# Attention, routing and two expert layers in one kernel: router logits of 19 of 24 chunks as fp16 products of rows turned by DMA, and preceding tokens counted per group

## The chip, the cores and the metric

One Trainium2 chip; the kernel runs on one of its cores. The metric is the device time of one execution in microseconds (us). A change of about 0.5% is what a measurement of this kernel can tell from none.

## The reference, cut to what matters

Gated linear attention over 4 batches, 8 heads, 768 steps and head size 48, then a mixture of 8 experts of which every token takes its best two by noisy logits, then a dense two-layer block. The change concerns `logits`, `noise_scale` and the places that the chosen tokens get in their expert's list.

```python
f = 1.0 / (1.0 + np.exp(-f_logit))
for t in range(S):
    state = f[:, :, t, :, None] * state + np.einsum('bhd,bhe->bhde', k[:, :, t], v[:, :, t])
    y[:, :, t] = np.einsum('bhd,bhde->bhe', q[:, :, t], state)
...
logits = x @ w_gate
noise_scale = np.log1p(np.exp(x @ w_noise))
noisy_logits = logits + noise_scale * noise
top2 = np.argpartition(-noisy_logits, 2, axis=1)[:, :2]
...
h = np.maximum(x[mask] @ w1[e], 0.0)
out[mask] += top2_w[mask, k, None] * (h @ w2[e])
...
h = x @ w_in
g = h - np.tanh(h)
return (g @ w_out).astype(np.float32)
```

## The kernel before, in words

The 3072 tokens are 24 chunks of 128 tokens: chunk j is step c = j // 4 of batch b = j % 4. The kernel has three stages. The first, some 180 us long, runs the attention chunk by chunk, routes the tokens and writes their rows into a DRAM list `xs` by expert. The second runs the experts from there, the third the dense block. The change lies in the first stage, and the order of all work there is written out by hand: each engine executes its instructions in the order in which the program issues them, and waits in place.

One pass of the main loop (`for j in range(NT)`) issues, in this order:

- `load_all(j + 3)`: on SP's queue the loads of `kq` (512 KB), `v` (192 KB) and, two chunks further ahead, `f` (256 KB); in passes 1 to 4 two `clear` writes of 288 KB each go behind them.
- `scores(j + 1)`: 8 fp32 products into two banks, and on DVE the masked copies `am` (L341).
- `scaled(j + 2)`: on ACT two exponentials (L320, L321), on DVE `kqT` for the keys (L323), on POOL `kqT` for the queries (L325).
- `post(...)`: on POOL two scatters (L479) of rows of chunks that are already routed; a scatter writes 128 rows of `x16`.
- `decay(j + 3)`: ACT (L310, L311) and on DVE the scan (L312).
- `logits(j - 1)` (L410): three fp32 products of `xT` with the two 16-column gate matrices (96 columns are streamed), and a copy of 16 columns to `lgs` on ACT (L411). If j - 1 is the last chunk of its group, `route` of that group is started as a generator.
- `outputs(j)`: 12 fp32 products into `pY` (L364, L366); ACT copies `pY` twice, to `x` in fp32 (L369) and to the high half of `x16` in fp16 (L371); DVE forms the low half from `x` and the high half (L372).
- `key_rows(j + 1)`, `states(j)` (L383, DVE L387, POOL L390).
- `x_transposed(j)`: three fp32 transposes of `x` on TensorE (L398) and a copy to `xT` on ACT (L400).
- between these, `advance(2)` takes two steps of the oldest started `route`; every second pass loads and splits a block of expert weights (`raw`, L144, L145).

`route` works on a group of four chunks (the last two groups have three and one): ACT makes the noise scale, DVE the best two per token and the mark `sel`; then `pre[:, j + 1]` adds up the marks of all chunks before, one small DVE addition per chunk (L440); two products on TensorE (L444, L445) give each token's place; more small DVE operations give the slots `yslot`, and 8 scatters are put on the list of `post`.

```python
for j in js:
    yield
    tt(pre[:, j + 1], pre[:, j], sel[:, j], op=OP.add)
for _ in range(2 if g < len(groups) - 2 else 1):
    yield
pos = ps.tile([128, 4, NE], F32, name="pt", tag="b7" if g > 4 else "b2")[:, :G]
nc.tensor.matmul(pos, before, sel[:, jj], start=True, stop=False)
nc.tensor.matmul(pos, ones, pre[:, jj], start=False, stop=True)
```

In the third stage `put_m` (L624) turns a 128 x 768 fp16 block by one DMA transpose from SP's queue, which is the shape that the change uses in the first stage. "Pass j" below is the j-th turn of the main loop; in the trace it is taken from the start of `scores(j + 1)` on TensorE to that of `scores(j + 2)`.

Of the kernel before, what the change touches and what calls it, by code (L numbers as in the profile page):

```python
# [23 lines left out]
NT = B * NCH  # L24
# [21 lines left out]
SM = 2.0 ** 12  # L46
SI = 2.0 ** 6
# [6 lines left out]
ISUM = (8.0, 1.0e8)  # L54
MSUM = (40.0, 1.0e9)
# [16 lines left out]
def fast(ctx, tc, flag, f_cols, kq_cols, v_rows, gates, blank, w12, w_in, w_out, out):  # L72
# [49 lines left out]
    pre = consts.tile([128, NT + 1, NE], BF, name="pre")  # L122
    nc.vector.memset(pre[:, 0, :], 0.0)

# [125 lines left out]
    with ExitStack() as actx:  # L250
# [106 lines left out]
        def outputs(j):  # L357
# [10 lines left out]
            x = work.tile([128, DM], F32, name="x")  # L368
            nc.scalar.activation(x, pY[:, :384], AF.Copy)  # L369
            x16 = xkeep[j // 4 % 3][:, j % 4, :]  # L370
            nc.scalar.activation(x16[:, :DM], pY[:, :384], AF.Copy, scale=SX)  # L371
            nc.vector.scalar_tensor_tensor(x16[:, DM:], x, SX, x16[:, :DM], op0=OP.mult, op1=OP.subtract)  # L372
            T["x", j], T["x16", j] = x, x16
# [20 lines left out]
        def x_transposed(j):  # L394
            x = T.pop(("x", j))
# [9 lines left out]
        group_of = {j: g for g, js in enumerate(groups) for j in js}  # L405
        def logits(j):
            p = ps.tile([128, 96], F32, name="pt", tag="b7")
            xT = T.pop(("xT", j))
            for a in range(3):
                nc.tensor.matmul(p, xT[:, a, :], gn[:, 16 * a:16 * a + 96], start=(a == 0), stop=(a == 2))  # L410
            nc.scalar.activation(lgs[:, j, :], p[:, :16], AF.Copy)  # L411
# [3 lines left out]
        def route(g):  # L415
# [5 lines left out]
            tt = nc.vector.tensor_tensor  # L421
            nl = small.tile([128, 4, NE], F32, name="nl")[:, :G]
# [15 lines left out]
            for j in js:  # L438
                yield
                tt(pre[:, j + 1], pre[:, j], sel[:, j], op=OP.add)  # L440
            for _ in range(2 if g < len(groups) - 2 else 1):
# [3 lines left out]
            nc.tensor.matmul(pos, ones, pre[:, jj], start=False, stop=True)  # L445
# [48 lines left out]
        warm(90)  # L494
        decay(0)
# [8 lines left out]
        decay(2)  # L504
        warm(30)
        for j in range(NT):
# [12 lines left out]
            if j:  # L519
                logits(j - 1)  # L520
                if j - 1 in ends:
                    chains.append(route(group_of[j - 1]))
# [7 lines left out]
            states(j)  # L530
            x_transposed(j)
# [193 lines left out]
    okay = consts.tile([128, 14], F32, name="okay")  # L725
# [17 lines left out]
    def checks():  # L743
# [4 lines left out]
        check(1, dv, 0.0, OP.is_lt)  # L748
        yield
# [3 lines left out]
        nc.tensor.matmul(count[:, 0], ones, pre[:, NT], start=True, stop=True)  # L753
        nc.tensor.matmul(count[:, 1], ones, pre[:, EARLY], start=True, stop=True)
        nc.tensor.matmul(count[:, 2], ones, pre[:, 4], start=True, stop=True)
# [365 lines left out]
```

## Time and profile before

| | |
|---|---|
| time, median of 3 runs | 971.24 us (967.05 to 971.27) |
| the profiled execution | 962.48 us, of which the span of the trace is 960.7 us |
| TensorE (PE) busy | 938.4 us, 98% |
| VectorE (DVE) busy | 616.0 us, 64% |
| ScalarE (ACT) busy | 611.2 us, 64% |
| GpSimd (POOL) busy | 160.5 us, 17% |
| DMA | 120.03 MB, mean 125 GB/s |
| passes 1 to 3 of the loop | 5.3 us each |
| passes 4 to 19 | 6.2 us each (scores at 33.64 to scores at 133.16) |

Shares over the whole span are averages over three stages with different limits, so the first stage has to be read by itself, and there by pass. The busy time of TensorE is modelled at its end, so that pass lengths are taken from starts of instructions.

### The profile page before, as it was taken

The page shows a single profiled execution, that of the slowest core. Times are in us where ns is not written, and L with a number is a line of the kernel's source. Part 1 is how long each engine was busy: PE and PEld are TensorE (multiplying, and loading weights), DVE is VectorE, ACT ScalarE, POOL GpSimd, SP SyncE. Part 2 cuts the span into 40 slices and gives each one's busy share as a digit, 9 for nine tenths or more (in the row PEclk, how much of TensorE's full clock was granted, in tenths as well). Part 3 has the DMA queues.
Part 4 walks back from the last instruction along what each step waited for, and adds up shares of the span by engine and source line. Part 5 has one row for each costly group of instructions (what it writes and reads, how often), then busy time and mean ns, then how long its engine had stood idle before and what let it go on. Part 6 is the DMA issues. An engine that isn't in the chain of part 4 may idle for free.

```text
span 960.7 us, 16309 instructions
## 1 busy us (share of the span) xinstructions
PE 938.4 (98%) x5970; PEld 576.5 (60%) x5970; DVE 616.0 (64%) x1274; ACT 611.2 (64%) x1593; POOL 160.5 (17%) x194
## 2 busy tenths in 40 slices
PE   8999998999999999999999999979999999999996
PEld 8999986555656565656556554535555555555553
DVE  8999995466464646566666556556566565665764
ACT  7777763575757575776767566666665666666663
POOL 2387786000000000000000223200301201000000
PEclk9999999999999999999999999989999999999999
DMA  7877855756565456564645354212222121110001
GB/s 274 286 248 252 263 166 170 200 176 167 153 177 149 161 143 187 151 157 134 186 122 136 99 149 103 64 34 44 74 42 47 44 58 42 42 26 1 33 1 37
DMA packets 111801, 120.03 MB, mean 125 GB/s; under 512 B 66400, under 2 KB 89568, under 8 KB 111584
## 3 DMA queue, kind: packets, MB, share of 16 engines
q1 hardware_dynamic: 105568, 100.03, 36.4%
q0 software_dynamic: 6144, 18.88, 6.3%
q8 instruction: 48, 0.79, 0.3%
q14 instruction: 41, 0.34, 0.1%
HBM read 76.41 MB, written 29.88 MB: 111 GB/s over the span
## 4 chain that ended last, share of the span: by engine, by line
PE 60%; ACT 21%; DVE 14%; issue 1%; DMA 1%; POOL 0%; SPq 0%; DVEq 0%; ACTq 0%
PE py L200 24%; PE ph L185 23%; ACT s L638 6%; DVE s L639 6%; DVE g L641 6%; ACT hs L647 5%; ACT z L637 5%; PE pY L366 4%; PE pA L339 2%; PE pt L410 2%; PE pY L364 2%; PE pK L383 2%; ACT junk L628 1%; ACT junk L149 1%; ACT g L614 1%
## 5 line engine op out<-in xcount | busy, mean ns | idle before, releaser
L200 PE MATMUL py<-wsplit,hs 128*128 128x384 f16 x2432 | 433.8, 327 | 7.2 <-ACT o L665 5.6
L200 PEld LDWEIGHTS <-hs 128*128 128x128 f16 x2432 | 237.0, 98 | 181.3 <-issue 9.2
L185 PE MATMUL ph<-xt,wsplit 128*128 128x512 f16 (+3 forms) x1152 | 223.5, 339 | 0.4 <-DMA xt<-xs 0.4
L185 PE MATMUL ph<-xt,winS 128*128 128x512 f16 x864 | 201.7, 379 | 0.0
L185 PEld LDWEIGHTS <-wsplit 128*128 128x128 f16 x1152 | 112.5, 98 | 86.7 <-DMA xt<-xs 0.8
L218 DVE SCALAR_TENSOR_TENSOR hs<-ph,hs 128x256 f16<-128x256 f32 (+2 forms) x192 | 79.6, 443 | 119.1 <-ACT hs L210 118.9
L608 POOL DMA_INDIRECT g<-y_rows,yslot x48 | 52.7, 1097 | 585.1 <-ACT wsplit L144 376.0
L210 ACT ACTIVATE hs<-ph 128x512 f16<-128x512 f32 (+3 forms) x128 | 65.8, 514 | 132.6 <-PE ph L185 132.6
L647 ACT ACTIVATE hs<-g 128x512 f16<-128x512 f32 x96 | 60.4, 629 | 138.5 <-DVE g L641 138.5
L185 PEld LDWEIGHTS <-winS 128*128 128x128 f16 x864 | 84.4, 98 | 92.0
L639 DVE SCALAR_TENSOR_TENSOR s<-s,z 128x512 f32<-128x512 f32 x96 | 66.5, 692 | 80.9 <-ACT s L638 80.9
L648 DVE TENSOR_TENSOR hs<-g,hs 128x512 f16<-128x512 f32 x96 | 66.4, 692 | 63.3 <-ACT hs L647 61.9
L145 DVE SCALAR_TENSOR_TENSOR wsplit<-raw,wsplit 128x768 f16<-128x768 f32 x72 | 70.3, 976 | 16.3 <-ACT wsplit L144 15.0
L149 ACT ACTIVATE junk<-wsplit 128x384 f16<-128x384 f16 x144 | 74.4, 516 | 2.3
L638 ACT ACTIVATE s<-z,bias_a 128x512 f32<-128x512 f32 x96 | 69.3, 722 | 3.1
L641 DVE SCALAR_TENSOR_TENSOR g<-s,ph 128x512 f32<-128x512 f32 x96 | 65.9, 687 | 3.3
L144 ACT ACTIVATE wsplit<-raw 128x768 f16<-128x768 f32 x72 | 59.9, 832 | 0.3 <-DMA raw<-wo_f 0.3
L479 POOL DMA_INDIRECT xs<-xkeep,yslot x48 | 55.7, 1161 | 15.8 <-issue 8.7
L637 ACT ACTIVATE z<-ph 128x512 f32<-128x512 f32 x96 | 55.4, 577 | 2.0 <-PE ph L185 1.9
L366 PE MATMUL pY<-v,am 128*128 128x48 f32 x384 | 53.3, 267 | 0.0
L366 PEld LDWEIGHTS pY<-v,am 128*128 128x128 f32 x384 | 49.6, 192 | 0.1
L325 POOL TENSOR_TENSOR kqT<-eneg,kq 128x512 f32<-128x512 f32 x23 | 32.0, 1392 | 16.0 <-ACT eneg L321 15.7
(135 smaller groups left out, 904.9 us busy)
## 6 DMA issues: line engine op xcount, KB each, us to landing
raw<-in_w SPq DMA_DIRECT2D x64, 384.0 KB, 3.8
kq<-in_kq_cols SPq DMA_DIRECT2D x24, 512.0 KB, 5.8
y_rows<-yo SPq DMA_DIRECT2D x47, 192.0 KB, 1.9
f<-in_f_cols SPq DMA_DIRECT2D x24, 256.0 KB, 4.3
w<-in_moe_w_out SPq DMA_DIRECT2D x32, 192.0 KB, 3.4
w<-in_moe_w_in SPq DMA_DIRECT2D x24, 256.0 KB, 3.4
v<-in_v_rows SPq DMA_DIRECT2D x24, 192.0 KB, 3.2
out<-o SPq DMA_DIRECT2D x24, 192.0 KB, 2.0
```

The source lines that it names most:

```text
L145: nc.vector.scalar_tensor_tensor(t[:, 1], raw, SW, t[:, 0], op0=OP.mult, op1=OP.subtract)
L149: nc.scalar.activation(junk[:, :DM], RING[e, f][:, 0, 3 * i:3 * i + 3, :].rearrange("p a b -> p (a b)"), AF.Square, accum_out=wsum[:, 8 * ...
L185: nc.tensor.matmul(ph[:, :n], l, x[:, r, :n], start=(o == 0), stop=(o == 8))
L200: nc.tensor.matmul(p[:max(m, 128)], l, r, start=(f == 0 and o == 0), stop=(f == last and o == len(ops) - 1))
L218: nc.vector.scalar_tensor_tensor(hs[:, at:at + hi - lo], ph[:, lo:hi], 0.0, hs[:, lo:hi], op0=OP.max, op1=OP.subtract)
L366: nc.tensor.matmul(pY[:, at + 48 * s:at + 48 * s + 48], am[:, s, a, :], vt[:, 2 * a + s, :], start=not c, stop=bool(s) or not c)
L637: nc.scalar.activation(z, ph, AF.Square, scale=SZ ** 0.5 / SH, accum_out=hsum[:, i:i + 1])
L638: nc.scalar.activation(s, z, AF.Square, scale=1.0 / SZ, bias=bias_a)
L639: nc.vector.scalar_tensor_tensor(s, s, ZD, z, op0=OP.add, op1=OP.mult)
L641: nc.vector.scalar_tensor_tensor(g, s, 0.5, ph, op0=OP.mult, op1=OP.mult)
L647: nc.scalar.activation(hs[:, :512], g, AF.Copy)
L648: nc.vector.tensor_tensor(hs[:, 512:], g, hs[:, :512], op=OP.subtract)
```

## The change

For the chunks 0 to 18 (`TURNED = 19`) the logits no longer come from the fp32 `x`. The fp16 pair `x16` (high and low half, 768 columns), which is made for the scatters anyway, is turned by one DMA transpose on SP's queue (`x_transposed`), and `logits_turned` multiplies the six turned blocks with the gate matrices in fp16: their high and low parts stand side by side in `g16` (3 x 32 columns), followed by zeros in `g_wide`, and each of the six products streams 192 columns, of which the first 32 are used. ACT copies 32 columns to `lg2`, and `route` adds high and low part. `x` in fp32 (ACT's copy L369) is made only for the chunks 19 to 23; for the others DVE reads `pY` itself. A chunk's logits come two passes after its outputs, before it was one; from chunk 19 on it stays one. `gates16` makes the fp16 gates before the loop. `pre` holds one sum per group: DVE sums a group's marks with one reduction and adds it, and the marks of earlier chunks of the same group enter by up to three further small products (`ones` times `sel`).

```diff
@@ outputs(j)
-            x = work.tile([128, DM], F32, name="x")
-            nc.scalar.activation(x, pY[:, :384], AF.Copy)
-            x16 = xkeep[j // 4 % 3][:, j % 4, :]
+            x16 = T["x16", j] = xkeep[j // 4 % 3][:, j % 4, :]
+            x = pY[:, :384]
+            if j >= TURNED:
+                x = T["x", j] = work.tile([128, DM], F32, name="x")
+                nc.scalar.activation(x, pY[:, :384], AF.Copy)
             nc.scalar.activation(x16[:, :DM], pY[:, :384], AF.Copy, scale=SX)
             nc.vector.scalar_tensor_tensor(x16[:, DM:], x, SX, x16[:, :DM], op0=OP.mult, op1=OP.subtract)
...
         def x_transposed(j):
+            if j < TURNED:
+                xT = T["xT", j] = work.tile([128, 6, 128], F16, name="xT16")
+                nc.sync.dma_start_transpose(xT, T["x16", j])
+                return
             x = T.pop(("x", j))
...
+        def logits_turned(j):
+            p = T["pt", j] = ps.tile([128, 192], F32, name="pt", tag="b7")
+            xT = T.pop(("xT", j))
+            for a in range(6):
+                at = 32 * (a % 3)
+                nc.tensor.matmul(p, xT[:, a, :], g_wide[:, at:at + 192], start=(a == 0), stop=(a == 5))
+
+        def chosen(j):
+            if j < TURNED:
+                nc.scalar.activation(lg2[:, j, :], T.pop(("pt", j))[:, :32], AF.Copy, scale=1.0 / (SX * SG))
+            else:
+                logits(j)
+            if j in ends:
+                chains.append(route(group_of[j]))
...
@@ route(g)
+            if j0 < TURNED:
+                t = slice(j0, min(j0 + G, TURNED))
+                tt(lgs[:, t, :], lg2[:, t, :16], lg2[:, t, 16:], op=OP.add)
+                yield
...
-            for j in js:
-                yield
-                tt(pre[:, j + 1], pre[:, j], sel[:, j], op=OP.add)
-            for _ in range(2 if g < len(groups) - 2 else 1):
+            yield
+            own_sum = small.tile([128, NE], BF, name="own_sum")
+            with nc.allow_low_precision("counts up to 24"):
+                nc.vector.tensor_reduce(own_sum, sel[:, jj].rearrange("p g e -> p e g"), axis=AX.X, op=OP.add)
+            tt(pre[:, g + 1], pre[:, g], own_sum, op=OP.add)
+            for _ in range(4 if g < len(groups) - 2 else 1):
                 yield
             pos = ps.tile([128, 4, NE], F32, name="pt", tag="b7" if g > 4 else "b2")[:, :G]
             nc.tensor.matmul(pos, before, sel[:, jj], start=True, stop=False)
-            nc.tensor.matmul(pos, ones, pre[:, jj], start=False, stop=True)
+            for i in range(1, G):
+                nc.tensor.matmul(pos[:, i:], ones, sel[:, j0 + i - 1, None, :].to_broadcast([128, G - i, NE]),
+                                 start=False, stop=False)
+            nc.tensor.matmul(pos, ones, pre[:, g, None, :].to_broadcast([128, G, NE]), start=False, stop=True)
...
+        def gates16():
+            for i in range(2):
+                d = g16[:, :, 16 * i:16 * i + 16]
+                if i:
+                    nc.vector.scalar_tensor_tensor(d, wgn, SG, g16[:, :, :16], op0=OP.mult, op1=OP.subtract)
+                else:
+                    nc.vector.tensor_scalar(d, wgn, SG, None, op0=OP.mult)
+            nc.scalar.activation(junk[:, :48].rearrange("p (a c) -> p a c", a=3), g16[:, :, :16], AF.Square,
+                                 accum_out=gsum)
...
         scaled(1)
         decay(2)
+        gates16()
         warm(30)
         for j in range(NT):
...
-            if j:
-                logits(j - 1)
-                if j - 1 in ends:
-                    chains.append(route(group_of[j - 1]))
+            if 2 <= j < TURNED + 2:
+                chosen(j - 2)
+            if j > TURNED:
+                chosen(j - 1)
...
             states(j)
+            if 0 < j <= TURNED:
+                logits_turned(j - 1)
             x_transposed(j)
```

The sum `gsum` is also tested at the end with the kernel's other range tests. On TensorE, one pass before: the fp32 transposes of `x`, then the scores of the next chunk, then the logits (`pA` are the score banks; fp32 weight loads are not listed apart).

```order
615 L383 MATMUL pK<-v,krows 128x96 x4
616 L398 MATMUL pE<-ident,x 128x128 x3
617 L339 MATMUL pA_1976<-kqT 128x128
618 L339 MATMUL pA_1977<-kqT 128x128
...
625 L410 MATMUL pt<-gn,xT 128x96 x3
626 L364 MATMUL pY<-st_161,kqT 128x96
627 L366 MATMUL pY<-v,am 128x48 x2
```

The same place after, in an earlier pass:

```order
577 L392 MATMUL pK<-v,krows 128x96 x4
578 L424 LDWEIGHTS xT_1223
579 L424 MATMUL pt<-g_103,xT_1223 128x192
...
588 L424 LDWEIGHTS xT_1223
589 L424 MATMUL pt<-g_103,xT_1223 128x192
590 L347 MATMUL pA_1313<-kqT 128x128
...
597 L347 MATMUL pA_1314<-kqT 128x128
598 L372 MATMUL pY<-st_162,kqT 128x96
599 L374 MATMUL pY<-v,am 128x48 x2
```

The transposes and the fp32 logits are gone; six fp16 products (of the chunk before) stand behind the state products. On SP's queue, two passes before:

```order
50 L135 DMA raw<-in_w 128x768
51 L265 DMA kq<-in_kq_cols 128x1024
52 L271 DMA v<-in_v_rows 128x384
53 L259 DMA f<-in_f_cols 128x512
54 L265 DMA kq<-in_kq_cols 128x1024
```

and after:

```order
64 L406 DMA_TRANSPOSE xT_1223<-xkeep_172 128x6x128
65 L273 DMA kq<-in_kq_cols 128x1024
66 L279 DMA v<-in_v_rows 128x384
67 L267 DMA f<-in_f_cols 128x512
68 L406 DMA_TRANSPOSE xT_1302<-xkeep_172 128x6x128
69 L143 DMA raw<-in_w 128x768
70 L273 DMA kq<-in_kq_cols 128x1024
```

Each pass has one transfer more on that queue, which waits for the low half of `x16` of that pass; the `kq` load of the next pass (and the `raw` load, where there is one) stands behind it. On DVE, where a group's route starts, after:

```order
115 L320 SCALAR_TENSOR_TENSOR fc<-carry,fc 128x512
116 L452 TENSOR_TENSOR lgs<-lg_106 128x64
117 L382 SCALAR_TENSOR_TENSOR xkeep_172<-pY,xkeep_172 128x384
118 L459 TENSOR_TENSOR nl<-ex,gn 128x32
...
123 L396 TENSOR_TENSOR tsum<-pK,st_163 128x384
124 L473 TENSOR_REDUCE own_sum<-sel 128x8
125 L474 TENSOR_TENSOR pre<-pre,own_sum 128x8
```

The sum of high and low logits stands behind the scan and ahead of the low half of `x16`; the four additions to `pre` have become a reduction and one addition.

## Rows read from the trace of the kernel before

**Rows 1.** Passes 1-4, 9-12: us, PE PEld DVE ACT POOL busy, clock, DMA share, GB/s

```profile
17.66:22.98 5.32, 5.32 (x54) 5.04 (x53) 5.32 (x8) 4.42 (x11) 2.06 (x2) 1.00 0.77 214
22.98:28.31 5.33, 5.33 (x54) 5.04 (x53) 5.29 (x9) 4.20 (x10) 2.06 (x2) 1.00 0.94 296
28.31:33.64 5.33, 5.33 (x55) 5.04 (x54) 4.78 (x9) 4.20 (x10) 2.10 (x2) 1.00 0.91 309
33.64:39.86 6.22, 6.22 (x63) 5.93 (x62) 4.68 (x9) 4.66 (x12) 2.11 (x2) 1.00 0.98 360
...
64.81:71.10 6.29, 6.29 (x65) 6.00 (x64) 6.18 (x19) 4.93 (x11) 4.30 (x6) 1.00 0.77 253
71.10:77.32 6.22, 6.22 (x63) 5.93 (x62) 6.08 (x17) 4.20 (x10) 4.85 (x7) 1.00 0.66 225
77.32:83.54 6.22, 6.22 (x63) 5.93 (x62) 5.58 (x10) 4.93 (x11) 5.34 (x7) 1.00 0.90 296
83.54:89.76 6.22, 6.22 (x63) 5.93 (x62) 4.76 (x10) 4.66 (x12) 5.30 (x7) 1.00 0.77 245
```

**Rows 2.** Timeline of PE in the pass from 102.27: start us, us, what

```profile
103.36 0.91 PE L410 MATMUL pt<-gn,xT 128*128 128x96 f32 x6
104.10 0.39 PE L364 MATMUL pY<-st,kqT 128*128 128x96 f32 x2
...
107.20 1.03 PE L383 MATMUL pK<-v,krows 128*128 128x96 f32 x8
108.07 0.49 PE L398 MATMUL pE<-ident,x 128*128 128x128 f32 x3
```

**Rows 3.** Timeline of PE before the loop

```profile
9.75 1.84 PE L492 MATMUL pK<-ones 128*128 128x128 bf16 x30
```

**Rows 4.** Chain that ended last, dense stage: start us, us, what

```profile
901.86 1.95 PE py L200 x12
```

**Rows 5.** Groups by line, 36 to 132 us: count, busy us, mean ns, idle before

```profile
L371 ACT ACTIVATE xkeep<-pY 128x384 f16<-128x384 f32 x15 | 7.3, 485 | 0.0
L440 DVE TENSOR_TENSOR pre<-pre,sel 128x8 bf16<-128x8 bf16 x16 | 5.1, 317 | 0.1
L429 DVE TENSOR_TENSOR nl<-nl,lgs 128x32 f32<-128x32 f32 x4 | 0.7, 184 | 0.0
```

**Rows 6.** Timeline of DVE, its three waits between 78 and 90 us

```profile
78.68 1.42 DVE L145 SCALAR_TENSOR_TENSOR wsplit<-raw,wsplit 128x768 f16<-128x768 f32 x1 [0.64 <-ACT wsplit L144]
...
84.73 1.29 DVE L341 TENSOR_TENSOR am<-pA,tri 128x512 f32<-128x512 f32 x2 [0.71 <-PE pA L339]
...
89.12 0.56 DVE L372 SCALAR_TENSOR_TENSOR xkeep<-x,xkeep 128x384 f16<-128x384 f32 x1 [0.75 <-ACT xkeep L371]
```

**Rows 7.** Tile xt, 560 to 900 us: the turned transfers on SP and their landing

```profile
L624 SPq DMA_TRANSPOSE xt<-m x22: 1211/1212/2164, 562.0 to 860.3; - x22
...
DMA to landing us min/median/max: 2.7/2.8/6.7
```

**Rows 8.** Stretches of the dense stage: one plain 192 KB store, one transfer L624

```profile
708.00:710.00 2.00, 2.00 (x11) 0.94 (x10) 1.80 (x4) 1.28 (x4) 0.00 (x0) 1.00 0.27 98
594.00:596.00 2.00, 2.00 (x13) 1.04 (x11) 1.38 (x2) 0.52 (x2) 0.00 (x0) 1.00 0.51 98
```

**Rows 9.** Timeline of SP's queue in the pass from 102.27

```profile
103.44 0.38 SPq L265 DMA_DIRECT2D kq<-in_kq_cols  x1
```

**Rows 10.** Tile kq, 0 to 140 us

```profile
DMA to landing us min/median/max: 3.6/5.8/8.4
```

**Rows 11.** Timeline before the loop: SP and ACT

```profile
8.60 0.33 SPq L500 DMA_DIRECT2D gn<-in_gates  x1
...
14.14 0.63 ACT L320 ACTIVATE epos<-fc 128x512 f32<-128x512 f32 x1 [1.29 <-DVE fc L312]
```

**Rows 12.** Tile gn

```profile
DMA to landing us min/median/max: 5.9/5.9/5.9
```

**Rows 13.** Chain that ended last, end of the first stage

```profile
168.83 3.78 DMA xs<-xkeep,yslot
```

More of the change, by code (lines that the diff above doesn't have):

```diff
@@ L46 @@
 SM = 2.0 ** 12
+SG = 2.0 ** 7
+TURNED = 19
 SI = 2.0 ** 6
@@ L54 @@
 ISUM = (8.0, 1.0e8)
+GSUM = (3.0, 1.0e8)
 MSUM = (40.0, 1.0e9)
@@ L121, in fast @@
     sel = consts.tile([128, NT, NE], BF, name="sel")
-    pre = consts.tile([128, NT + 1, NE], BF, name="pre")
+    pre = consts.tile([128, 8, NE], BF, name="pre")
     nc.vector.memset(pre[:, 0, :], 0.0)
+    g_wide = consts.tile([128, 256], F16, name="g16")
+    nc.vector.memset(g_wide[:, 96:], 0.0)
+    g16 = g_wide[:, :96].rearrange("p (a c) -> p a c", a=3)
+    gsum = consts.tile([128, 1], F32, name="gsum")
+    lg2 = consts.tile([128, TURNED, 32], F32, name="lg2")
     ring = ctx.enter_context(tc.tile_pool(name="ring", bufs=16))
@@ L367, in outputs @@
                                      start=not c, stop=bool(s) or not c)
-            x = work.tile([128, DM], F32, name="x")
-            nc.scalar.activation(x, pY[:, :384], AF.Copy)
-            x16 = xkeep[j // 4 % 3][:, j % 4, :]
+            x16 = T["x16", j] = xkeep[j // 4 % 3][:, j % 4, :]
[3 more added lines that the diff above has]
+                nc.scalar.activation(x, pY[:, :384], AF.Copy)
             nc.scalar.activation(x16[:, :DM], pY[:, :384], AF.Copy, scale=SX)
             nc.vector.scalar_tensor_tensor(x16[:, DM:], x, SX, x16[:, :DM], op0=OP.mult, op1=OP.subtract)
-            T["x", j], T["x16", j] = x, x16
         def states(j):
@@ L724, in fast @@
     dctx.close()
-    okay = consts.tile([128, 14], F32, name="okay")
+    okay = consts.tile([128, 15], F32, name="okay")
     held = small.tile([128, NT * NE], F32, name="held", bufs=1)
@@ L748, in checks @@
         check(1, dv, 0.0, OP.is_lt)
+        check(14, gsum, GSUM[0], OP.is_ge)
+        check(14, gsum, GSUM[1], OP.is_le)
         yield
@@ L752, in checks @@
         count = ps.tile([128, 3, NE], F32, name="pt", tag="b7")
-        nc.tensor.matmul(count[:, 0], ones, pre[:, NT], start=True, stop=True)
-        nc.tensor.matmul(count[:, 1], ones, pre[:, EARLY], start=True, stop=True)
-        nc.tensor.matmul(count[:, 2], ones, pre[:, 4], start=True, stop=True)
+        nc.tensor.matmul(count[:, 0], ones, pre[:, 7], start=True, stop=True)
+        nc.tensor.matmul(count[:, 1], ones, pre[:, EARLY // 4], start=True, stop=True)
+        nc.tensor.matmul(count[:, 2], ones, pre[:, 1], start=True, stop=True)
         total = consts.tile([128, 3], F32, name="total")
```

## The prediction

> **What bounds the kernel now.** I read the table of stretches first, cut at the passes of the loop [rows 1]. TensorE fills every pass: its weight loads alone are busy 5.93 of 6.22 us, at a granted clock of 1.00, that is 2.4 GHz. So passes 4 to 19 last 6.22 us and passes 1 to 3 last 5.33 us because TensorE needs them. But DVE is close behind: in passes 9 and 10 it is busy 6.18 of 6.29 and 6.08 of 6.22 us, and in passes 1 and 2 all but 0.04 us. POOL takes at most 5.34 us of a pass. The DMA engines are also well filled: 0.77, 0.94, 0.91 and 0.98 in passes 1 to 4, and 0.66 to 0.90 later. A shorter TensorE pass therefore meets DVE and DMA soon, and that decides the size of the gain.
>
> What a pass saves is handed on to the end of the stage: the chain goes there through the last scatter and the read of its rows [rows 13], and POOL's scatters start when the slots of chunks 16 to 19 are ready, in pass 21.
>
> **TensorE.** The logits take it from 103.36 to the first output product at 104.10, and the transposes from 108.07 to the end of the pass at 102.27 + 6.22 = 108.49 [rows 1, 2]: 0.74 + 0.42, of which some 0.04 is switching between products, so 1.12 us go. Six fp16 products come. No row has 192 columns: 30 products of 128 columns take 1.84 us, 0.061 each [rows 3], and 12 of 384 columns 1.95 us, 0.162 each [rows 4]; between them lies 0.061 + 64/256 x 0.101 = 0.086, six are 0.52 (bounds 0.37 and 0.97). Two small products for places become five in a group of four: three more at 0.061, 0.05 per pass. Net 1.12 - 0.52 - 0.05 = 0.55 us. Passes 9 to 12 take 24.95 us, 6.24 each, so **TensorE could go down to 5.69 us**.
>
> **DVE.** Passes 9 to 12 hold 6.18 + 6.08 + 5.58 + 4.76 = 22.60 us of work [rows 1]. Four additions to `pre` at 0.317 go (1.27); a reduction, an addition and the sum of high and low logits come, each at about the 0.184 of a small operation (0.55) [rows 5]: 22.60 - 0.72 = 21.88. Reading `pY` in place of `x` I cost at nothing: the operation keeps its 384 columns (bounds -0.2 and +0.2 us a pass). DVE also waits three times in these passes [rows 6]. The wait of `wsplit` for ACT (0.64) goes, because ACT loses two copies like L371's 0.485 a pass in front of it [rows 5]; that for the scores (0.71) goes, because TensorE is ahead by 0.55. The third (0.75) stays and grows: where a group's route starts, ACT's exponentials now wait for the new sum on DVE, which stands behind the scan, and ACT's high half of `x16` stands behind those exponentials; two exponentials of small operations' length and the copy of 0.485, with three handovers, make some 1.2 us (bounds 0 and 1.6). So **DVE needs (21.88 + 1.2) / 4 = 5.77 us a pass**, more than TensorE's 5.69.
>
> **SP and DMA.** A turned transfer occupies SP's queue for 1.21 us and lands 2.8 us after its issue in the quiet third stage, 6.7 at worst [rows 7]. The three loads of a pass take it about 0.38 each [rows 9], so its own time is not the limit. In DMA time one costs 0.51 x 2 us = 1.02 us, while a plain store of the same 192 KB costs 0.27 x 2 = 0.54 [rows 8]. Passes 9 to 12 hold 0.77 x 6.29 + 0.66 x 6.22 + 0.90 x 6.22 + 0.77 x 6.22 = 19.3 us of DMA work; with four transfers 23.4, or 5.85 us a pass. That is as much as DVE's 5.77, so I take **5.8 us a pass**. The Trainium skill (Advanced Engine Details and Errata, X-Bar Transpose (TRN2)) says that these transposes are as fast as regular DMAs, 350 to 400 GB/s; from that I estimate 0.5 us each and 5.3 us a pass, DMA no limit at all. The trace does not agree: 1.02 against 0.54 us for the same bytes.
>
> Two deadlines follow. The low half of `x16` is written at 89.12 + 0.56 = 89.68, when the pass ends at 89.76 [rows 1, 6]; its transfer is issued there, and its product stands 0.5 us before the end of the next pass, so it has 5.8 - 0.5 = 5.3 us to land. The `kq` load, before at 1.2 us into a pass [rows 9], stands behind it and is issued some 1.6 us into the next one; DVE reads it in the pass after, when `am` is done, at 84.73 + 1.29 = 86.02 or 2.5 us into a pass [rows 1, 6]: it has 5.8 + 0.9 = 6.7 us, against 5.8 at the median and 8.4 at worst [rows 10]. Both fit at the median.
>
> **Ahead of the loop.** `gates16` needs `gn`, which is issued at 8.60 and lands at 14.50 [rows 11, 12]. DVE is done with its scan at 14.1 and makes the two operations until 14.9, ACT its square until 15.3, while its exponential started at 14.14 before. The chain through the keys of chunk 2 moves by 1.2 us, less the 0.42 of the transposes: a loss of 0.8 (bounds 0 and 1.2).
>
> **The early passes.** Passes 1 to 4 hold 0.77 x 5.32 + 0.94 x 5.33 + 0.91 x 5.33 + 0.98 x 6.22 = 20.1 us of DMA work in 22.2 us; with four transfers 24.1, over by 1.9. DVE is full there too, so nothing is gained; I take half of the excess as lost, 0.9 (bounds: a gain of 1.5, a loss of 1.9).
>
> **The sum.** Passes 5 to 17: 13 x (6.24 - 5.80) = 5.7. Passes 18 and 19, where the loads run out: 2 x 0.55 = 1.1. Against that 0.8 and 0.9. From pass 20 on the fp32 path is as before, and the steps of `route` up to the slots are as many; nothing is counted. Together -5.1 us: the profiled execution's 962.48 would be 957.4. The median of the runs stands 8.76 us above that execution, and the same difference is kept: 971.24 - 5.1 = **966.1 us**. A change of 0.5%, 4.9 us, is about what a measurement can tell from none, so this is at its edge.
>
> **The rivals.**
> - *TensorE sets the pace and all of its time comes back.* DVE's third wait vanishes too, since ACT makes one copy less ahead of the high half; then DVE needs 21.88 / 4 = 5.47 us and TensorE's 5.69 decides. For it: that wait is ACT's, and ACT is busy 4.93 us at most [rows 1]. Against it: the exponentials' new wait for DVE, and DMA at 5.85. 19 x 0.55 - 0.8 = 9.7 us less: 961.5.
> - *DMA cannot be filled.* Passes 9 to 12 at 23.4 us of work and a share of 0.95, which the passes before the change reach singly but not in a row, last 6.16 us. Then 13 x 0.08 + 1.1 - 0.8 - 1.9 = -0.6 us of gain: 971.8, no change.
> - *The turned rows come late, and the loop is slower.* TensorE waits in place for `xT`, and scores, outputs and states of the next chunks stand behind that product. A pass lasts at least the landing plus 0.5 us; from a landing of 5.7 us on it is longer than now. At the 5.8 us of the `kq` loads, which share the engines with it, a pass lasts 6.3 us: 13 x 0.06 more, and in passes 1 to 3, where two writes of 288 KB go ahead of it, 3 x 0.97; with the 0.8 that is +4.5: 975.7. Each further 0.1 us of landing costs 1.9 us. For it: the 6.7 us at worst in a quiet stage. Against it: the median of 2.8. The Trainium skill (VectorE: DVE Perf Modes, Rules for kernel authors, and The three transpose paths) speaks for this rival: 128x128 transposes belong on TensorE if PSUM will do, and by DMA one takes 1309 ns; six in a row would be an estimated 7.9 us. The trace does not agree: six blocks land in 2.8 us.
>
> **Chances.** DVE and DMA together set the pace, as forecast: 0.36, of which 0.21 falls beyond -0.5%. TensorE's pace: 0.22, all faster. DMA full: 0.24, of which 0.03 faster, 0.18 same and 0.03 slower. Rows late: 0.18, of which 0.16 slower. So faster 0.46, same 0.35, slower 0.19. The range goes from 959.0 (all of TensorE's time, and products at their lower bound, 19 x 0.15 more) to 976.5 (rows late by a little); a landing much above 5.8 us is left out.
>
> **What would show it.** Right: passes of 5.7 to 5.9 us from pass 5 on with DVE busy over 94% of them, DMA shares near 1 there, first scores of the loop's second pass near 18.4 us, passes 1 to 3 not shorter than 5.3, and the last scatter some 5 us earlier. Wrong: TensorE waiting for `xT` in its chain of waits, the low half of `x16` or `kqT` waiting for a DMA, or passes of 5.69 with TensorE full. The step most likely to fail is the DMA price of a turned transfer among loads, which the first stage has never shown.

## The result and the profile after

The change is slower: 980.96 us at the median of 14 runs (970.85 to 991.68) against 967.15 for the kernel before (14 runs); the ratio is 1.0125, with a 95% interval of 1.0095 to 1.0156. It leaves out the two longest runs of the change (991.68 and 986.38), as slow ones. The forecast was 966.1. The profiled execution took 985.25 us, its span 983.3, at a mean granted clock of 0.974 (before: 962.48, 960.7, 0.994).

Of single executions one thing must be known to read the rest: the mean granted clock differs from run to run, in both kernels. In the three traces compared below a fall of some 7 us near 650 us is in all; the one that differs lies from pass 20 on. The change's runs at a mean of 0.993 took 970.85 and 973.57 us, the one at 0.965 took 991.68; the kernel before has about 0.990 at the median, and its eleven runs at 0.993, taken with the experiments below, took 964.85 to 969.38, 968.0 in the mean. From these runs I estimate that some 4 us of the loss stand at an equal mean clock, and that the other 10 go with the clock. Since it varies, I traced the kernel before a second time (last experiment but two, 967.10 us, clock 0.989) and compare with both traces. Starts of `scores` on TensorE and of the first second-layer product of the experts (`py`), in us from the timelines:

| start | before | before, second trace | after |
|---|---|---|---|
| pass 0 | 13.00 | 13.25 | 13.78 |
| pass 5 | 39.86 | 40.11 | 41.67 |
| pass 17 | 114.71 | 114.95 | 116.65 |
| pass 20 | 133.16 | 133.41 | 135.87 |
| pass 21 | 139.58 | 139.82 | 146.02 |
| first `py` | 161.48 | 165.94 | 183.39 |
| span | 960.7 | 965.3 | 983.3 |

From pass 0 to pass 20 the loop gains nothing and loses 1.9 us against the first trace; pass 20 alone loses 3.7 (10.15 against 6.42). Until the experts start 15 us more go against the first trace, 11 against the second. After that the lag stays at some 22 and 18.

The stretches that answer to [rows 1], passes 1 to 4 and 9 to 12 of after (length, then busy time of PE, PEld, DVE, ACT, POOL, then the granted clock, the DMA share and GB/s):

```profile
18.22:24.30 6.08, 5.07 (x51) 4.56 (x51) 6.08 (x9) 3.89 (x9) 2.08 (x2) 1.00 0.58 96
24.30:30.14 5.84, 5.00 (x52) 4.56 (x51) 5.15 (x9) 4.55 (x11) 2.25 (x3) 1.00 1.02 312
30.14:35.73 5.59, 4.99 (x51) 4.55 (x50) 4.40 (x7) 3.17 (x9) 1.92 (x2) 1.00 1.10 331
35.73:41.67 5.94, 5.89 (x59) 5.45 (x59) 4.82 (x8) 2.76 (x7) 2.10 (x2) 1.00 1.12 300
...
66.73:72.94 6.21, 5.89 (x59) 5.45 (x58) 4.47 (x8) 3.52 (x9) 4.26 (x7) 1.00 1.05 323
72.94:79.25 6.31, 6.11 (x64) 5.60 (x64) 5.61 (x17) 4.46 (x11) 3.89 (x6) 1.00 1.10 226
79.25:85.96 6.71, 5.89 (x60) 5.45 (x59) 6.57 (x18) 4.16 (x9) 5.00 (x6) 1.00 1.04 316
85.96:92.45 6.49, 5.88 (x59) 5.45 (x58) 6.11 (x10) 3.53 (x8) 5.80 (x10) 1.00 0.99 305
```

TensorE has 0.3 us less to do in a pass and is no longer full, but passes 9 to 12 are 6.2 to 6.7 us long. What it and its neighbours wait for, up to 140 us (table of waits: us in total, times, longest):

```profile
ACT wsplit L152 <- DMA raw<-in_w: 10.8, 8, 1.9
PEld L424 <- DMA xT<-xkeep: 8.3, 12, 1.5
ACT ex L456 <- DVE lgs L452: 7.6, 4, 1.9
PE pt L424 <- DMA xT<-xkeep: 6.3, 11, 1.4
DVE wsplit L153 <- ACT wsplit L152: 4.9, 4, 1.4
```

Three new waits: TensorE for the turned rows, ACT (and DVE behind it) for the weight loads, ACT for DVE's new sum. The turned row of chunk 15 shows how the first comes about: pass 16 starts at 110.45, and only then does DVE write the low half, and SP issue the transfer (timelines of DVE and of SP's queue):

```profile
111.44 0.53 DVE L382 SCALAR_TENSOR_TENSOR xkeep<-pY,xkeep 128x384 f16<-128x384 f32 x1
```

```profile
111.99 1.22 SPq L406 DMA_TRANSPOSE xT<-xkeep  x1
113.27 0.57 SPq L143 DMA_DIRECT2D raw<-in_w  x1
```

The chain that ended last goes through such a transfer into pass 19 (start, us, what), and then TensorE and ACT hold each other up in pass 20 (their timelines, wait in brackets):

```profile
129.61 5.29 DMA xT<-xkeep
134.95 0.67 PE pt L424 x6
```

```profile
135.87 1.16 PE L347 MATMUL pA<-kqT 64*128 64x128 f32 x16
138.92 0.91 PE L438 MATMUL pt<-gn,xT 128*128 128x96 f32 x6 [1.88 <-ACT lg L428]
...
142.56 0.23 ACT L456 ACTIVATE ex<-lgs 128x32 f32<-128x32 f32 x1 [2.52 <-DVE lgs L452]
```

The fp32 logits of chunk 19 wait for their bank, since ACT copies chunk 18's logits behind five long operations; then ACT waits for DVE's sum, and the outputs' copies stand behind that. The sum is late because DVE's `kqT` ahead of it takes 2.89 us (0.68 in pass 21), while POOL runs two operations from 138.54 to 140.60; before, it took 3.17 us in this pass, but the exponentials of `route` needed no sum and ran at 136.79 without a wait. From DVE's timeline:

```profile
138.27 2.89 DVE L331 SCALAR_TENSOR_TENSOR kqT<-epos,kq 128x512 f32<-128x512 f32 x1
...
142.29 0.18 DVE L452 TENSOR_TENSOR lgs<-lg 128x48 f32<-128x48 f32 x1
```

TensorE is busy 2.12 of 4 us, and after that the granted clock is down:

```profile
132.00:136.00 4.00, 3.71 (x35) 3.38 (x36) 4.00 (x7) 1.73 (x7) 3.63 (x6) 1.00 1.14 261
136.00:140.00 4.00, 2.12 (x26) 1.93 (x26) 3.80 (x5) 2.97 (x8) 3.76 (x5) 1.00 0.83 318
140.00:144.00 4.00, 4.00 (x22) 4.00 (x20) 2.47 (x4) 0.51 (x3) 3.38 (x7) 0.50 0.17 64
...
176.00:180.00 4.00, 4.00 (x15) 2.17 (x13) 1.18 (x6) 1.07 (x3) 0.00 (x0) 0.50 0.01 4
180.00:184.00 4.00, 4.00 (x25) 2.63 (x24) 0.97 (x4) 1.53 (x6) 3.17 (x6) 0.88 0.27 98
```

For some 40 us TensorE runs at 1.2 GHz in place of 2.4: `scores` takes 2.08 us where it took 1.16. In the first trace of before it stays at 2.4 GHz there:

```profile
136.00:140.00 4.00, 2.77 (x27) 2.44 (x28) 4.00 (x4) 2.55 (x8) 3.81 (x5) 1.00 0.27 101
140.00:144.00 4.00, 4.00 (x44) 3.88 (x41) 3.86 (x14) 1.22 (x3) 2.67 (x5) 1.00 0.26 98
```

### The profile page after: what moved, and what is told of

Same layout as the page of the kernel before. It is cut to its first block, busy times and chain, and to the rows that moved or that the text cites. A ratio compares the mean times of both kernels' runs of the same rounds, so it can differ in the third digit from the quotient of the medians.

```text
span 983.3 us, 16216 instructions
## 1 busy us (share of the span) xinstructions
PE 950.8 (97%) x5930; PEld 585.5 (60%) x5930; DVE 614.3 (62%) x1278; ACT 597.4 (61%) x1557; POOL 157.0 (16%) x194
## 4 chain that ended last, share of the span: by engine, by line
PE 52%; ACT 20%; DVE 18%; issue 4%; DMA 3%; POOL 1%; SPq 0%; DVEq 0%; POOLq 0%
PE py L208 24%; PE ph L193 24%; DVE s L689 6%; DVE g L691 6%; ACT s L688 5%; ACT hs L697 5%; ACT z L687 5%; DMA kq<-in_kq_cols 2%; DVE am L349 2%; DVE fc L320 1%; ACT junk L678 1%; ACT junk L157 1%; DMA xT<-xkeep 1%; PE pY L374 1%; DVE kqT L331 1%
## 5 line engine op out<-in xcount | busy, mean ns | idle before, releaser
L193 PE MATMUL ph<-xt,wsplit 128*128 128x512 f16 (+3 forms) x1152 | 226.0, 342 | 0.0
L152 ACT ACTIVATE wsplit<-raw 128x768 f16<-128x768 f32 x72 | 60.0, 833 | 11.0 <-DMA raw<-in_w 10.8
L374 PE MATMUL pY<-v,am 128*128 128x48 f32 x384 | 60.0, 288 | 0.4 <-DVE xkeep L382 0.4
L374 PEld LDWEIGHTS pY<-v,am 128*128 128x128 f32 x384 | 56.6, 215 | 1.0 <-DVE xkeep L382 0.6
L516 POOL DMA_INDIRECT xs<-xkeep,yslot x48 | 51.1, 1066 | 30.5 <-DVE yslot L501 21.3
L372 PE MATMUL pY<-st,kqT 128*128 128x96 f32 x160 | 38.6, 327 | 1.1 <-issue 0.8
```

Of the source, the lines that this page charges most:

```text
L193: nc.tensor.matmul(ph[:, :n], l, x[:, r, :n], start=(o == 0), stop=(o == 8))
L374: nc.tensor.matmul(pY[:, at + 48 * s:at + 48 * s + 48], am[:, s, a, :], vt[:, 2 * a + s, :], start=not c, stop=bool(s) or not c)
```

## The experiments

"Pass length" is the mean of passes 6 to 18, from the starts of passes 6 and 19: 6.24 us before, 6.34 after; it is of one traced execution each. Ratios are to runs of the kernel before that were taken with each.

**Either half of the change alone.** The first kernel has the counting only (the diff's hunks at `pre`, `own_sum` and the products for `pos`). The second adds to the kernel before

```
+            if j < 19:
+                nc.sync.dma_start_transpose(work.tile([128, 6, 128], F16, name="xT16"), T["x16", j])
```

> The kernel before, with the counting per group alone (no turned rows). All theories agree here: DVE loses 0.72 us in four passes, TensorE gets 0.05 us a pass more, and TensorE sets the pace: 0 to 1 us slower than before, no fall of the granted clock near 140 us. A result more than 4 us slower would put the loss on the counting, against all of them.

> The kernel before, with 19 turned transfers beside it that nothing reads. Theory 1 (the DMA engines are full, so loads come late): the DMA share of passes 5 to 17 rises by 0.16 to about 0.95 to 1.05, wsplit and kqT wait for loads, and the kernel is 2 to 6 us slower than before; the granted clock stays at 1.00, since TensorE keeps its fp32 work. Rival (only TensorE's own wait for the turned rows costs): no more than 1 us slower.

Counting: 969.58 us, ratio 0.9995 (0.9970 to 1.0020). Unread transfers: 970.30, 0.9992 (0.9967 to 1.0017). Neither costs anything that these intervals could tell. Two rows of the table of stretches, before and with the transfers, 13 passes each:

```profile
46.15:127.22 81.07, 81.07 (x801) 77.33 (x800) 73.88 (x170) 60.37 (x142) 62.51 (x78) 1.00 0.75 247
```

```profile
49.62:130.69 81.07, 81.07 (x801) 77.33 (x800) 74.82 (x170) 60.80 (x142) 61.83 (x78) 1.00 1.04 278
```

The share rises from 0.75 to 1.04 and the passes last 6.24 us as before. So the first theory's 2 to 6 us fell: a share of 1.04 does not by itself lengthen a pass of 6.24 us; an engine has to wait for something that comes late.

**The wait in pass 20.** Once the bank is changed, once the wait is filled with work:

```
+            p = ps.tile([128, 96], F32, name="pt", tag="b2" if j == TURNED else "b7")
```

```
+            if j == TURNED + 1:
+                warm(30)
```

> The change, with the first fp32 logits (chunk 19) in another PSUM bank, so that they don't wait for ACT's copy of chunk 18's logits in pass 20 (1.88 us there). Theory 2 (that wait alone lets the granted clock fall to 0.50): the clock stays at 1.00 until the dense stage and the time falls by 10 to 14 us against the change, to 967 to 971. Theory 1 (several late loads and rows together leave TensorE idle in passes 17 to 20): the fall comes all the same, 977 to 982.

> The change, with 30 products of ones (1.84 us before the loop) in pass 20 between the scores and the fp32 logits, where TensorE waits 1.88 us. Theory 2: as with the other bank, the granted clock stays at 1.00, 967 to 971. Theory 1: TensorE has also been idle in passes 17 and 19, the clock falls all the same or falls later, 976 to 982. If the clock had nothing to do with TensorE being idle, the time would be that of the change plus 0 to 2 us.

Bank: 983.32, 1.0137 (1.0095 to 1.0178). TensorE's wait of 1.88 us went, but ACT then stood 3.87 us in its wait for DVE's sum and TensorE 3.21 behind it; the clock fell at 142 us. Fill: 976.84, 1.0079 (1.0049 to 1.0110); the clock stays at 1.00 up to 160 us and then falls for some 8 us. Theory 2 fell as put (taking that wait away only makes room for the next), but with TensorE's gap filled the fall comes later and 4 us come back.

**What holds the passes.** Product one pass later; weight loads one pass earlier; DVE's scan behind the low half; rows turned by TensorE. The core of each:

```
-            if 0 < j <= TURNED:
-                logits_turned(j - 1)
+            if 1 < j <= TURNED + 1:
+                logits_turned(j - 2)
```

```
+            if 2 <= j < 18 and not j % 2:
+                load_weights(0, (j - 2) // 2)
             x_transposed(j)
-            if 3 <= j < 19 and j % 2:
-                load_weights(0, (j - 3) // 2)
```

```
             outputs(j)
+            scan(j + 3)
```

```
+                for a in range(6):
+                    nc.tensor.transpose(p[:, a, :], T["x16", j - 1][:, a * 128:(a + 1) * 128], ident16)
+                nc.scalar.activation(xT, p, AF.Copy)
```

> The change with each turned product one pass later (18 turned rows, three buffers for them, the first two fp32 logits in another bank), so that a row has a whole pass more to land. Theory A (TensorE, waiting in place for rows that DVE finishes 1 to 2 us into the next pass and that land 4 to 6 us after, is what holds the passes at 6.2 us): the waits for turned rows go, passes 4 to 17 last 5.8 to 6.0 us, the loop ends 4 to 5 us earlier, and the time is 974 to 978 against the change's 981. Theory B (late weight loads hold ACT and DVE) and theory C (DVE's own work, 5.9 us a pass, is the floor): passes stay at 6.1 to 6.3 us, 979 to 983.

> The change with each weight load issued one pass earlier, ahead of the turned transfer. Theory B (ACT waits 10.8 us in the loop for these loads and DVE 4.9 behind it): those waits go and passes 4 to 19 fall by 0.2 to 0.3 us, 975 to 978. Theory A: the rows are as late as before, passes stay at 6.2 us, 979 to 983.

> The change with DVE's scan (1.21 us) moved behind the low half of the row, so that the turned transfer is issued up to 1.2 us earlier in each pass. Theory A: most of TensorE's 4.3 us of waits for turned rows go, passes last 5.9 to 6.1 us, 976 to 979. Theory B or C: no difference, 979 to 983. If DVE then waits for the outputs before that low half, in a loop where it has nothing to spare, passes grow by up to 0.5 us: 985 to 990.

> The change with the rows turned by TensorE in place of DMA: six fp16 transposes a chunk, one pass after the row is written, one ACT copy of 768 columns, the six fp16 products where the fp32 logits stood. TensorE: 6 x 0.061 + 0.52 + 0.05 = 0.94 us against 1.16 before, so passes of 6.0 us if TensorE sets them and 19 x 0.22 = 4 us less than before: 963 to 967. If DMA and rows that come late are all of the change's loss (theories A and B), it lies at or below the kernel before. If DVE's 5.9 us and its waits are the floor (theory C), 968 to 972. If the hand-over to fp32 in passes 19 to 21 with its fall of the clock is the loss whatever turns the rows: 975 to 982.

| kernel | median us | ratio (95%) | pass length | ACT's wait for the sum in pass 20 |
|---|---|---|---|---|
| product later | 981.28 | 1.0147 (1.0097 to 1.0198) | 6.19 | 3.53 |
| loads earlier | 981.55 | 1.0148 (1.0083 to 1.0212) | 6.13 | 2.60 |
| scan later | 984.39 | 1.0140 (1.0077 to 1.0204) | 6.17 | 0.57 |
| turned by TensorE | 974.15 | 1.0074 (1.0047 to 1.0102) | 6.34 | 3.86 |

The first three gain only 0.15 to 0.2 us a pass, and the time does not move: the next wait is close behind, and all keep the hand-over of pass 20. The one with earlier loads pays at once besides: in its trace TensorE waits 2.14 us for a turned row in pass 3 (0.60 in the change), the clock then falls to 0.50, and pass 4 lasts 10.50 us in place of 5.94. The last kernel gains nothing in the passes, but without a single turned transfer the loss is still 7 us, so much of it need not be DMA's. The 963 to 967 that were expected of it if TensorE set the passes did not come.

**ACT's wait for the sum.** With the other bank,

```
                 tt(lgs[:, t, :], lg2[:, t, :16], lg2[:, t, 16:], op=OP.add)
-                yield
+                for _ in range(3):
+                    yield
```

> The change with the other bank for chunk 19's fp32 logits and with the group's exponentials two steps of the route later, so that ACT copies the outputs (x, high half) before it waits for DVE's new sum of high and low logits. Theory D (in pass 20 ACT stands 2.5 to 3.5 us in that wait, with TensorE behind it for the copy of chunk 20's rows, and the granted clock falls there): TensorE's wait in pass 20 is under 1 us, the next pass starts 2 to 3 us earlier, the clock stays at 1.00 past 148 us, and the time is 969 to 975. If the fall of the clock does not depend on that wait, 978 to 983.

974.64, 1.0055 (1.0028 to 1.0082): pass 20 takes 5.70 us in place of 10.15, the pass length is 6.16, and the clock falls only after 152 us. The pass ahead of it takes 1.4 us more (7.56 against 6.12; TensorE waits 1.73 us for its row). Against the change's 980.96 that is 6.3 us of the 13.8 (by the ratios 6.8 of 12.1) for these two waits of the hand-over, for the bank and for the sum.

**DVE's work.** Weight loads early, and the low half of the first expert's weights left out (ACT writes the high half twice):

> The change with early weight loads, and with DVE's low half of the first expert's weights left out: ACT writes the high half twice in its place, so 0.48 us a pass less for DVE, 0.25 more for ACT. Theory C (DVE sets the pass: 5.83 us of work and 0.30 of waits, 6.13 together in the kernel with early loads): passes 7 to 19 fall to 5.65 to 5.8 us. Theory A (rows that come late): passes stay at 6.0 to 6.2 us. The time itself is told by what the clock does behind the loop: 970 to 982.

Pass length 6.08: only 0.06 less than with early loads, so theory C fell; DVE's own work is not the floor. Only the first stage can be read here: the 8558 us hold the general path too, which the kernel takes when its sums leave their bounds.

**Filling the kernel before, and all mends at once.** The first adds `warm(9)` ahead of and behind the fp32 transposes in passes 20 to 23 and `warm(10)` ahead of the last logits; the second joins later products, early loads, later exponentials, `gall` by ACT, and these fillings.

> The kernel before, with products of ones where TensorE waits in passes 20 to 23 (18 a pass, 10 ahead of the last logits; 0.061 us each). If the kernel before, too, loses time in executions where the granted clock falls behind the loop (its clock is 0.994 in the profiled run and about 0.988 at the median), this one stays at 0.99 or above and is 2 to 5 us faster, 963 to 967 against 968 to 970. If the fall doesn't depend on TensorE's gaps there: no difference, or up to 2 us slower.

> The change with all that helped singly: products one pass later, early weight loads, exponentials two steps later, other bank, gall by ACT in place of DVE (0.154 us a pass), products of ones in passes 20 to 23. If DVE's work and ACT's wait in pass 20 are what is left (theories C and D), passes 7 to 18 last 5.9 to 6.0 us, the loop ends 3 to 4 us ahead of the kernel before, and the time is 962 to 968. If a turned transfer costs by itself: 970 to 978.

Filled: 974.45, 1.0068 (1.0041 to 1.0095): the fillings cost 5 us, where at most 2 were expected; behind them ACT reads the logits of chunk 22 at 157.05 us, 3.6 us after TensorE's record of them ends. All together: 978.58, 1.0106 (1.0072 to 1.0141), but the pass length is 5.78. In these passes the loop does reach the forecast's pace, and pass 20 starts at 132.02, 1.1 us ahead of before. Behind it (timeline of PE):

```profile
148.66 2.08 PE L347 MATMUL pA<-kqT 64*128 64x128 f32 x16 [4.11 <-POOL spacer L516]
...
167.59 0.20 PE L479 MATMUL pt<-sel,before 128*128 128x24 bf16 x1 [3.94 <-DVE sel L469]
```

The first wait: eight scatters now stand on POOL ahead of the last queries (in the change five, before two), since routing ends later. The second: in the change the group of chunks 20 to 22 has two steps fewer, so its product for places comes ahead of the first expert product on TensorE, which waits there instead of working.

**The hand-over mended.** Without fillings; the steps are given back, and the scatters kept off the last queries:

```
-            for _ in range(4 if g < len(groups) - 2 else 1):
+            for _ in range({5: 3, 6: 1}.get(g, 2)):
...
-            post({18: 3, 19: 3, 20: 8, 23: 4}.get(j, 2))
+            post({20: 2, 21: 8, 23: 4}.get(j, 2))
```

> As the kernel with all that helped singly, without the products of ones; the slots of chunks 20 to 22 counted behind the first expert product again, as before the change, and no more than two scatters ahead of the keys and queries of the last chunk (there TensorE waited 4.1 us for POOL). If what is left is the hand-over behind pass 20 (theory D): passes 7 to 18 at 5.75 us as there, the loop ends 1 to 3 us ahead of the kernel before, TensorE waits under 1 us at a time up to the slots, the granted clock falls no more than in the kernel before, and the time is 962 to 968. If turned transfers cost by themselves, or the fall of the clock comes whatever the waits are: 972 to 979.

> The change with early weight loads, other bank, exponentials two steps later, slots of chunks 20 to 22 behind the first expert product, at most two scatters ahead of the last keys and queries; turned products where the change has them. Theory A (rows late for the product in the next pass) would leave passes at 6.1 us and the loop's end 1 to 2 us behind the kernel before: 969 to 973. If the row's lateness is made up by DVE's shorter waits: passes of 5.9 us and 964 to 968.

> The rows turned by TensorE with the same mends (early loads, exponentials later, gall by ACT, slots behind the first expert product, scatters). TensorE's own 6.0 us a pass and no turned transfers: 963 to 968 if the hand-over was its loss; 972 to 976, as it was without the mends, if not.

> The kernel before, unchanged, for a second trace: its profiled execution had a granted clock of 0.994, its runs about 0.989 at the median. All theories: within 2 us of 969; if the trace's clock is near 0.988, a stretch at 0.50 between 148 and 170 us, 8 to 16 us long, where the first trace has none.

All mends at once: 980.25, 1.0106 (1.0071 to 1.0141); the change with its products where they are, mended: 974.68, 1.0053 (1.0027 to 1.0079); rows turned by TensorE, mended: 972.12, 1.0037 (1.0015 to 1.0058). None reaches the 962 to 968 that were expected if the hand-over was the loss. Pass lengths are 5.95, 5.87 and 6.22. The second starts pass 20 at 130.67, 2.5 us ahead of before; so the later product isn't needed. Its waits in passes 6 to 18 (all of DVE's, then all of TensorE's):

```profile
DVE am L349 <- PE pA L347: 1.9, 4, 0.7
```

```profile
PE pt L424 <- DMA xT<-xkeep: 1.0, 1, 1.0
```

But behind the loop all three lose it again; in the second kernel:

```profile
160.15 0.80 PE L438 MATMUL pt<-gn,xT 128*128 128x96 f32 x6
...
169.94 0.18 ACT L439 ACTIVATE lgs<-pt 128x16 f32<-128x16 f32 x1 [5.05 <-remote]
...
172.99 0.19 PE L479 MATMUL pt<-sel,before 128*128 128x8 bf16 x1 [9.11 <-DVE sel L469]
```

The second trace of before (967.10) shows that the kernel before loses time there as well, though less; these stretches ran at 1.00 in its first trace, and the experts start 4.5 us later. The first row is from the first trace, the others from the second:

```profile
148.00:152.00 4.00, 2.78 (x24) 2.42 (x23) 1.31 (x3) 1.36 (x3) 3.00 (x5) 1.00 0.69 252
...
148.00:152.00 4.00, 2.96 (x25) 2.60 (x24) 1.48 (x3) 1.24 (x3) 2.61 (x5) 1.00 0.73 250
152.00:156.00 4.00, 3.82 (x19) 3.82 (x20) 0.67 (x5) 0.76 (x4) 3.34 (x7) 0.57 0.41 146
156.00:160.00 4.00, 4.00 (x18) 3.15 (x18) 0.15 (x1) 0.87 (x2) 2.77 (x6) 0.50 0.44 167
160.00:164.00 4.00, 4.00 (x21) 2.49 (x20) 2.74 (x16) 1.07 (x3) 0.00 (x0) 0.65 0.05 17
```

**The scatters as in the change.** The last two undo the line with `post` in the second and third of these and nothing else.

> The mended kernel (turned by DMA) with the scatters handed out as in the change: five ahead of the last keys and queries, four fewer in a row behind the loop. There the loop ended 2.5 us ahead of the kernel before, and TensorE then did nothing for 9 us, with scatters in a row on POOL. If the row of scatters makes that gap: it shrinks to the 2 us of the kernel before, and the time is 964 to 969. If not (the gap comes from how the last slots hang together): 972 to 976.

> The same for the kernel whose rows TensorE turns: five scatters ahead of the last keys and queries. It has TensorE gaps of 0.4 to 1.7 us at 170 to 178 us that nothing in the profile releases. If the row of scatters makes them: 964 to 968, at or below the kernel before. If not: 970 to 975.

966.65, 0.9986 (0.9960 to 1.0013), and 969.99, 1.0006 (0.9979 to 1.0033). In the first the gap of 9 us is gone, and the time is as expected. The second gains only 2 us, and what was expected if the scatters were the reason (964 to 968) did not come. So the change with three mends (loads, exponentials with their bank, steps of the last group but one) is level with the kernel before, 14 us below the change; its fastest run, 961.36, is below every run of before beside it (962.56). A version clearly faster than the kernel before was not found.

Up to pass 17 the two mended kernels that turn rows by DMA are the same program, and pass 4 starts alike in their traces (36.78 and 36.79); there they part, which prices a fall of the clock. The one with the change's scatters, then the other:

```profile
34.00:36.00 2.00, 0.31 (x3) 0.15 (x2) 1.15 (x3) 1.81 (x5) 0.77 (x1) 1.00 1.07 217
36.00:38.00 2.00, 1.81 (x16) 1.66 (x18) 0.00 (x0) 0.86 (x3) 0.46 (x2) 0.70 1.04 393
38.00:40.00 2.00, 2.00 (x16) 1.78 (x12) 1.11 (x2) 0.00 (x0) 0.86 (x1) 0.50 1.10 383
```

```profile
34.00:36.00 2.00, 0.81 (x8) 0.65 (x6) 1.61 (x3) 1.85 (x5) 0.31 (x1) 1.00 1.22 221
36.00:38.00 2.00, 1.81 (x23) 1.54 (x24) 0.02 (x1) 1.21 (x4) 0.90 (x2) 1.00 1.04 393
38.00:40.00 2.00, 2.00 (x19) 2.00 (x20) 2.00 (x5) 0.00 (x0) 0.89 (x1) 1.00 1.06 374
```

Both wait for a turned row ahead of pass 4 (1.87 and 1.38 us) at DMA shares of 1.04 to 1.22. In the first TensorE was busy 0.31 of 2 us, the clock falls, and pass 4 lasts 10.56 us; in the second it was busy 0.81 of 2, the clock stays, and the pass lasts 6.25. So this fall costs 4.3 us.

It is no single case: of the six traces with turned transfers and loads a pass earlier, four have a fall there and a pass 4 of 9.4 to 10.6 us; of the six with the loads where the change has them, none has. So the earlier loads give back about 4 us at the start in most of these executions, and this was not mended. In the trace of the mended kernel with the change's scatters pass 20 starts at 136.87, later than in the change; what makes it level with the kernel before is what was mended from pass 20 on. Its pass length, too, is 6.01 where the same program had 5.87: passes 8 and 9 last 6.6 to 6.7 us, with short waits for rows.

## Why the prediction was wrong

- **"From pass 20 on the fp32 path is as before, and the steps of `route` up to the slots are as many; nothing is counted."** This step failed, and it is most of the miss: the execution that was forecast would start pass 20 at 133.16 - 5.1 = 128.1 and take 957.4; the traced one (4 us above the median) starts it at 135.87 and takes 985.25, so 8 us of the miss of 28 lie ahead of pass 20 and 20 behind. The hand-over from turned to fp32 logits puts a wait for a bank and one for DVE's sum into pass 20; the last group but one has two steps fewer, against "as many"; the scatters move behind by a pass. The exponentials' wait for the sum was foreseen, but priced at 1.2 us on DVE; in pass 20 it is 2.5 us on ACT with TensorE behind it, and up to 3.9 in the variants. Mending the two waits gave 6.3 us, with the loads and the steps 14. Of a fall of the clock the prediction said nothing. TensorE's waits in pass 20 are 1.9 and 0.6 us, the lag in the trace 18 to 22 us; that the 40 us at 1.2 GHz make most of this is argued from the clock of the runs (above), as no experiment holds the clock.
- **"Both fit at the median."** The deadlines failed on their start. The row in the chain lands 5.3 us after its issue, as allowed, but the row of chunk 15 is issued 1.5 us into the next pass, where the prediction had it at the end of its own: a TensorE that has less to do runs ahead of DVE, and the low half is DVE's. The `raw` load on that queue was given no deadline at all; ACT waited 10.8 us for it and DVE 4.9 behind ACT.
- **DMA, 5.85 us a pass.** The price was mis-sized and the rule around it wrong: among loads a turned transfer takes (1.04 - 0.75) x 81.07 / 13 = 1.8 us of DMA share, not 1.02 [rows 8]; yet at a share of 1.04 a mended pass lasts 5.87 us. A share near 1 is no wall by itself in these kernels; what costs is an engine that waits for a late transfer. The Trainium skill (Advanced Engine Details and Errata, X-Bar Transpose (TRN2)) has these transposes as fast as regular DMAs; 1.8 against 0.54 us for the same bytes disagrees more than before, but with the transfers unread it costs no time.
- **DVE, 5.77 us.** Mis-sized. In the change DVE has 74.25 / 13 = 5.71 us of work in passes 6 to 18, where 5.47 was forecast, and 7.3 / 13 = 0.56 of waits for ACT, where 0.30 was; together 6.27 of 6.34. The additions to `pre` were costed at their mean of 0.317 [rows 5], but most take 0.16, and one in a group waits for POOL (before; after):

```profile
115.95 1.01 DVE L440 TENSOR_TENSOR pre<-pre,sel 128x8 bf16<-128x8 bf16 x2
116.12 0.82 POOL L390 TENSOR_TENSOR st<-tsum,gall 128x384 f32<-128x384 f32 x1 [1.95 <-DVE pre L440]
```

```profile
100.85 0.83 POOL L399 TENSOR_TENSOR st<-tsum,gall 128x384 f32<-128x384 f32 x1 [2.26 <-DVE tsum L396]
100.91 0.78 DVE L474 TENSOR_TENSOR pre<-pre,own_sum 128x8 bf16<-128x8 bf16 x1
```

  Both end as POOL's operation ends (116.96 and 116.94; 101.69 and 101.68), and the one addition that is left keeps that wait. The Trainium skill (SBUF — State Buffer, section SBUF: two separate sides) says that a DVE operation with two SBUF inputs and a GpSimd operation that reads SBUF lock each other out for a whole instruction; these rows agree. So a group saved 0.1 us instead of 0.72. In the mended kernel DVE has 72.76 / 13 = 5.60 us of work and 0.15 of waits. That the two add up to nearly 5.77 is luck: work and waits of an engine make up nearly its pass whatever sets it, and here TensorE does. That reading `pY` costs nothing was right (0.535 us against 0.541).
- **TensorE, 5.69 us.** Nearly right: in the mended kernel it is busy 75.25 of 76.25 us, 5.79 a pass, and sets the pace, as the first rival had it; in the change it is busy 5.90 of 6.34. The six products took 0.59 (116.06 to the next scores at 116.65), not 0.52.
- **Ahead of the loop, -0.8.** Wrong: `gates16` costs nothing here. Pass 1, where the loss should show, starts 0.56 us later in the trace after (18.22), but the first scores of all already start 0.79 later (8.95 against 8.16); from these it is 9.27 us against 9.50. The sign "near 18.4 us" came true by luck.
- **Early passes, -0.9.** About right: passes 1 to 4 take 23.45 us against 22.20, and 24.5 in two traces that are the same program up to pass 20 (other bank, filled wait).
- **The rivals.** The nearest was that the turned rows come late (975.7): its mechanism is there, 0.1 us a pass where it had 0.06, but it ended at the loop; that its time is the nearest is luck. "The step most likely to fail" was named as the DMA price; it failed, and did not matter. The lower end of the range works out at 961.5 - 19 x 0.15 = 958.7, not 959.0; nothing hangs on it.

## What to carry to other kernels

When a step that feeds several engines is replaced for all rows but the last, cost the pass where the old and the new way meet as a stage of its own: which bank both use, which small operation now stands ahead of a long one, and what was ordered by counting steps. Give every load that is queued behind a new transfer its own deadline, counted from when the producing engine really finishes once the bound engine is faster. A short wait of TensorE is to be priced at what a fall of the clock may cost behind it (4.3 us for one of 1.9 us here), not at its length alone.

## What was not expected of the hardware

- After TensorE had been busy 2.12 of 4 us the granted clock was 0.50 from 140 to about 181 us; after 2.77 of 4 us at 136 to 140 us in the first trace of before it stayed at 1.00. But the busy share does not decide it: at 148 to 152 us TensorE was busy 2.78 of 4 us in the first trace of before and the clock stayed, and 2.96 of 4 in the second, with no gap over 0.64 us, and it fell. The same program fell in one execution and not in another.
- The DMA share reads 1.22 in a stretch of 2 us, and 1.04 over 81 us, with passes no longer than at 0.75.
- Left open: why the other order of the scatters costs 8 us (974.68 against 966.65), with 20 in place of 16 behind POOL's last queries; of the 20, 14 stand in a row, while the 16 all do, so the length of the row alone does not explain it. With the 20 ACT waits 5 us for logits that TensorE's record ends at 160.95, with a releaser that the profile lists only as remote; filling TensorE in the kernel before gave a like gap of 3.6 us. What delays them was not tried further.
